# Block-sparse attention feeding a Swish MLP on one core: batch 0's block sums of V, both heads of a pair in one matmul

## The chip, the core and the metric

The kernel runs on one core of one Trainium2 chip. The core has five engines that work side by side: TensorE (PE) with its separate weight loads (PEld), VectorE (DVE), ScalarE (ACT), GpSimd (POOL) and SyncE (SP), and DMA queues. The metric is the device time of one execution in microseconds. The kernel before takes 212.0 us, the median of three runs (211.83 to 213.88).

## What is computed

An attention over four batches of eight heads (768 positions, 64 numbers per head) mixes a narrow window of near positions with 24 block summaries: the maximum of each block of 32 keys, and the mean of each block of 32 values. Its output goes through a two-layer MLP with a Swish between.

```python
    block, window = (32, 16)
    k_sum = k.reshape(B, H, nb, block, D).max(axis=3)
    v_sum = v.reshape(B, H, nb, block, D).mean(axis=3)
    ...
    scores_all = np.concatenate([scores_l_m, scores_s], axis=-1)
    ...
    v_all = np.concatenate([v, v_sum], axis=2)
    return np.matmul(a, v_all).astype(np.float32)
```

```python
    h = x @ w_in
    g = h * (1.0 / (1.0 + np.exp(-beta * h)))
    return (g @ w_out).astype(np.float32)
```

## The kernel before

Heads go in four pairs per batch. For each pair the values lie in `ve` as chunks of 128 rows, shifted by 16 positions, so that a head's 768 positions touch seven chunks (`NC = 7`; the two heads of a pair stand six chunks apart, `nch = 6`). The block sums of a head are seven matmuls, one per chunk, of the stationary matrix `A_avg[:, c]` (128 rows by 32 columns, a one where the row belongs to the block) with the chunk's 64 columns, accumulated in PSUM. Since the stationary matrix has 32 columns, such a matmul uses a strip of 32 of the PE array's 128 columns; `tile_position=(0, n)` says which strip, and the result lands on the 32 PSUM rows of that strip.

There are two routines for these sums. `mean_v` (L374) serves batches 1 to 3: it takes the two heads of a pair in one matmul (128 columns) and puts the four pairs on the four strips, chunk by chunk, 28 matmuls in all. `sum_v` (L384) serves batch 0 and takes one pair per call, because the pairs' values arrive one after the other in the first 20 us: 14 matmuls, head 0 and head 1 in turn, each on a strip of its own (strips 0 and 32 for pairs 0 and 2, 64 and 96 for pairs 1 and 3). Two copies per pair (L388, on DVE for pairs 0 and 1, on ACT for pairs 2 and 3) bring the sums from PSUM into `vd`, where head h of the pair has rows of its own. `blk0` (L466) multiplies `vd` with the block weights; `own0` (L454) and `edge0` (L460) add the near positions.

The order is written out by hand for the first stage: each engine does its work in the order of the calls, and an instruction that waits holds everything behind it on its engine. On PE that order is scores of pair 2, `sum_v(0)`, scores of pair 3, `sum_v(1)`, `own0` of pairs 0 and 1, `scores_blk(1)`, `blk0` and `edge0` of pairs 0 and 1, `sum_v(2)`, `own0`, `edge0`, `blk0` of pair 2, the small transpose of beta (L248), `sum_v(3)`, `own0(3)`, `edge0(3)`, `turn_x` (transposes, L491), `blk0(3)`, another `turn_x`, and then the first MLP matmuls (`h_dots`, L613). The values themselves are loaded by POOL's DMAs, one per pair (L116), ahead of the weights of the MLP.

From about 20 us on, PE goes from one block of matmuls to the next: the first MLP layer (L613, L643), the second (L664, L695), and between them the attention of the next batch (scores L508 and L525, values L570, sums L374).

Of the kernel before, what the change touches and what calls it, by code (L numbers as in the profile page):

```python
# [12 lines left out]
def kernel(  # L13
# [10 lines left out]
    nc = tc.nc  # L24
    ctx.enter_context(tc.manual_schedule(engines={getattr(mybir.EngineType, e) for e in ("SP", "Pool", "PE", "DVE", "Activation")}))
    P = 128
    f32 = mybir.dt.float32
# [4 lines left out]
    B, H, S, D = q.shape  # L32
# [4 lines left out]
    nch = S // P  # L37
    NC = nch + 1
# [41 lines left out]
    PC = 2 * nch  # L80
    ve_bufs = [const.tile([P, HC + 1, VW], bf16, name=f"ve{i}") for i in range(2)]
# [54 lines left out]
    A_avg = const.tile([P, NC, 32], bf16, name="A_avg")  # L136
# [7 lines left out]
    vd_bufs = [const.tile([P, 4, VW], bf16, name=f"vd{i}") for i in range(2)]  # L144
# [139 lines left out]
    def take(name, dt=f32):  # L284
        n = pools["n"]
        return pools["pool"].tile([P, n, 512 if dt == f32 else 1024], dt, name=name, tag="big", bufs=6 // n)
# [4 lines left out]
    def psum(shape, dt, name, tag):  # L291
        if tag == "t":
            return ps.tile(shape, dt, name=name, tag="t", bufs=2)
        flat = take(name, dt)[:, 0, 0:math.prod(shape[1:])]
        if len(shape) == 2:
            return flat
        return flat.rearrange("p (a b) -> p a b", b=shape[2])
# [80 lines left out]

    def sum_v(g, copy=dve):
        lo = HP * (g % 2)  # L380
        vm_ps = psum([P, D], f32, "vm_ps", "t")
        for c in range(NC):
            for h in range(2):
                nc.tensor.matmul(vm_ps[lo + 32 * h:lo + 32 * h + 32], A_avg[:, c], ve_bufs[0][:, PC * g + nch * h + c, 0:D],  # L384
                                 start=(c == 0), stop=(c == NC - 1), tile_position=(0, lo + 32 * h))
        for h in range(2):
            r = slice(lo + 32 * h, lo + 32 * h + 32)
            copy(out=vd_bufs[g // 2][r, 2 * (g % 2) + h, 0:D], in_=vm_ps[r])  # L388

    def rows_v0(g, copy=pool):  # L390
        for h in range(2):
# [318 lines left out]
    for nm, t, copy, src in (("k", qk_bufs["k"][:, 0:2], dve, k_f32), ("q", q0_bufs[0][:, 0:2], act, q_f32)):  # L710
        nat[(nm, 0, 0)] = t
        copy(out=t.rearrange("p h f -> p (h f)").rearrange("p (j h d) -> p h j d", h=2, d=D),
             in_=src.rearrange("p h (j d) -> p h j d", d=D))
# [17 lines left out]
    max_k(0, 2)  # L731
    scores0(2)
    sum_v(0)
    scores0(3)
    max_k(0, 3)
    sum_v(1)
    more_constants()
    open_av((0, 0, 2))
# [6 lines left out]
    edge0(1)  # L745
    norm_x((0, 0, 2))
    sum_v(2, act)
    open_av((0, 2, 1))
    own0(2, True)
# [81 lines left out]
    for b in range(B):  # L831
# [6 lines left out]
        main, t = [], 0.0  # L838
# [33 lines left out]
        if b == 0:  # L872
# [23 lines left out]
            for g in pairs:  # L896
                t = dn0 + OT * TK[g] if g < 2 else up1 + TK[g]
# [15 lines left out]
        elif nxt < B:  # L913
            for g in pairs:
                t = (2.6, 6.5, 10.4, 14.3)[g]
# [60 lines left out]
```

## Time and profile before

| | before |
|---|---|
| three runs, median (lowest to highest) | 212.0 us (211.83 to 213.88) |
| the profiled execution, its own time | 212.08 us |
| its span, first to last instruction | 210.4 us |
| PE busy | 204.0 us, 97% of the span |
| DVE, ACT, POOL busy | 110.5, 118.6, 80.5 us |
| L384, the sums of batch 0 | 56 matmuls between 12.0 and 17.6 us |

The rows of the profile give an instruction's start in us from the span's first instruction, and what engine, line and tile it belongs to. A matmul's duration counts from its first column until its result is in, so matmuls that follow each other overlap in these rows; how fast they go is read from the distance of their starts.

### The profile page before, as it was taken

What the parts mean: (1) busy time and instruction counts of PE and PEld (TensorE: products, weight loads), DVE (VectorE), ACT (ScalarE), POOL (GpSimd) and SP (SyncE); (2) the same over time, 40 slices, a digit from 0 to 9 for tenths busy, and PEclk for the clock granted to TensorE, in tenths of its full rate; (3) what the DMA queues carried; (4) which work ended last, traced back from release to release, by engine and by line L of the source; (5) the groups of instructions that cost most, each with busy time, mean ns of one, the idle gap of its engine ahead of it and who ended that gap; (6) DMA issues with size and microseconds to landing.
All of it is one profiled execution on the core that took longest, in us unless ns stands there. A gap on an engine that the chain in (4) does not pass through costs nothing.

```text
span 210.4 us, 4961 instructions
## 1 busy us (share of the span) xinstructions
PE 204.0 (97%) x2044; PEld 113.1 (54%) x2044; DVE 110.5 (53%) x311; ACT 118.6 (56%) x170; POOL 80.5 (38%) x116
## 2 busy tenths in 40 slices
PE   7998999999999999999999999999999999999993
PEld 2566654456555556565555456655545565654452
DVE  4887998987959868323926667524425000002120
ACT  3684988159697386668336266669165176640000
POOL 7997997593063399676300092000000000000000
PEclk9999999999999999999999999999999999999999
DMA  6999999999949999999999899900342500001212
GB/s 158 170 154 206 201 204 203 193 155 226 142 73 157 125 182 134 148 151 153 157 191 151 128 153 151 185 13 0 118 110 76 152 2 3 0 0 51 100 53 100
DMA packets 92055, 26.46 MB, mean 126 GB/s; under 512 B 81136, under 2 KB 89088, under 8 KB 92032
## 3 DMA queue, kind: packets, MB, share of 16 engines
q0 software_dynamic: 63888, 13.34, 78.7%
q1 hardware_dynamic: 27792, 12.40, 32.4%
q10 hardware_dynamic: 352, 0.39, 0.6%
q8 instruction: 16, 0.26, 0.5%
q14 instruction: 7, 0.06, 0.1%
HBM read 27.27 MB, written 6.29 MB: 160 GB/s over the span
## 4 chain that ended last, share of the span: by engine, by line
PE 85%; DMA 8%; POOL 3%; DVE 1%; issue 0%; ACT 0%
PE o_ps L664 35%; PE h_ps L613 32%; PE o_ps L695 5%; DMA qt<-q_all 4%; DMA ve<-in_v_dram 4%; PE h_ps L643 4%; PE av_ps L570 3%; PE s_ps L525 2%; POOL ve L116 1%; PE s_ps L508 1%; PE px L491 1%; POOL q L103 1%; PE vm_ps L374 0%; DVE qt L309 0%; PE av_ps L560 0%; POOL near L155 0%
## 5 line engine op out<-in xcount | busy, mean ns | idle before, releaser
L613 PE MATMUL h_ps<-xT,w_in_sb 128*128 128x384 bf16 x464 | 76.7, 326 | 0.0
L664 PE MATMUL o_ps<-w_out_sb,h_sb 128*128 128x512 bf16 (+2 forms) x352 | 75.8, 370 | 0.0
L625 ACT ACTIVATE h_sb<-h_ps,beta_sb 128x768 bf16<-128x768 f32 (+1 forms) x80 | 59.2, 775 | 23.2 <-PE h_ps L613 19.4
L613 PEld LDWEIGHTS <-w_in_sb 128*128 128x128 bf16 x464 | 45.0, 98 | 29.8
L664 PEld LDWEIGHTS <-h_sb 128*128 128x128 bf16 x352 | 32.6, 98 | 35.6
L683 DVE COPY o_sb<-o_ps 128x512 f32<-128x512 f32 x5 | 3.5, 691 | 38.6 <-PE o_ps L664 38.6
L551 DVE TENSOR_TENSOR attn<-attn,band 128x768 bf16<-128x768 bf16 x24 | 13.0, 555 | 17.3 <-ACT attn L500 15.6
L683 ACT COPY o_sb<-o_ps 128x512 f32<-128x512 f32 x15 | 8.9, 596 | 22.4 <-PE o_ps L664 17.2
L110 POOL DMA_DIRECT2D q_all<-in_q_dram x24 | 20.1, 858 | 3.5 <-DMA ve<-in_v_dram 2.8
L500 ACT ACTIVATE attn<-s_ps 128x768 bf16<-128x768 f32 x24 | 17.7, 814 | 3.6 <-PE s_ps L525 2.2
L116 POOL DMA_DIRECT2D ve<-in_v_dram x16 | 16.6, 1053 | 5.1 <-DMA w_out_sb<-in_moe_w_out_dram 3.6
L110 POOL DMA_DIRECT2D k_all<-in_k_dram x16 | 13.7, 870 | 3.7 <-DMA ve<-in_v_dram 2.4
L346 DVE TENSOR_TENSOR half<-kw 128x384 bf16<-128x384 bf16 x16 | 5.8, 365 | 16.5 <-DMA kw<-k_all 16.4
L367 DVE COPY vo<-ve 64x780 bf16<-64x780 bf16 (+3 forms) x30 | 11.4, 381 | 0.7
L580 DVE TENSOR_TENSOR x_nat<-av_ps,r 128x768 bf16<-128x768 f32 x12 | 11.5, 957 | 0.5
L695 PE MATMUL o_ps<-w_out_sb,h_sb 128*128 128x512 bf16 x48 | 11.6, 380 | 0.1
L676 ACT COPY o_sb<-o_ps 128x384 f32<-128x384 f32 x1 | 0.5, 480 | 19.0 <-PE o_ps L664 19.0
L244 ACT ACT_TABLE_LOAD x7 | 9.0, 1283 | 0.1
L643 PE MATMUL h_ps<-xT,w_in_sb 128*128 128x384 bf16 x48 | 8.3, 326 | 0.0
L356 DVE COPY kw<-kw 128x192 bf16<-128x192 bf16 (+2 forms) x32 | 8.3, 306 | 0.0
L493 ACT COPY xT<-px 128x384 bf16<-128x384 bf16 (+1 forms) x5 | 3.0, 608 | 8.0 <-PE px L491 8.0
L403 DVE COPY vo<-vm 32x780 bf16<-32x780 bf16 x12 | 7.4, 616 | 0.2
(125 smaller groups left out, 193.8 us busy)
## 6 DMA issues: line engine op xcount, KB each, us to landing
out_dram<-o_sb SPq DMA_DIRECT2D x23, 256.0 KB, 3.1
ve<-in_v_dram POOLq DMA_DIRECT2D x12, 192.0 KB, 6.5
q_all<-in_q_dram POOLq DMA_DIRECT2D x24, 96.0 KB, 7.7
w_in_sb<-in_moe_w_in_dram POOLq DMA_DIRECT2D x8, 256.0 KB, 8.5
k_all<-in_k_dram POOLq DMA_DIRECT2D x16, 96.0 KB, 6.8
w_out_sb<-in_moe_w_out_dram POOLq DMA_DIRECT2D x4, 256.0 KB, 6.7
w_out_sb<-in_moe_w_out_dram POOLq DMA_DIRECT2D x2, 512.0 KB, 8.9
k_all<-in_k_dram POOLq DMA_DIRECT2D x5, 192.0 KB, 9.0
```

The costliest lines, as they stand in the source:

```text
L110: nc.gpsimd.dma_start(out=t[:, :, h], in_=(k_row if nm == "k" else q_row)[b, g, :, h])
L116: nc.gpsimd.dma_start(out=ve_bufs[b % 2][:, lo:hi, 0:D], in_=src)
L367: copy(out=dst, in_=src)
L500: nc.scalar.activation(out=at[(b, g)][:, par].rearrange("p m h f -> p h m f"), in_=sv, func=ACTF.Exp, scale=scale)
L551: nc.vector.tensor_mul(out=a, in0=a, in1=band[:, par])
L580: nc.vector.tensor_mul(out=x.rearrange("p m h d -> p h m d"), in0=ov[:, :, :, 0:D], in1=r[:, :, :, None].to_broadcast([P, 2, n, D]))
L613: nc.tensor.matmul(big[:, j, 0:MG], w_in_sb[:, ki, ni * P:(ni + 1) * P], xT[b][:, ki, tok:tok + MG], start=(ki == 0), stop=(ki == k1 - 1))
L625: nc.scalar.activation(out=hb.rearrange("p (k m) -> p k m", m=MG), in_=big[:, j:j + w, 0:MG], func=ACTF.Silu, scale=beta_sb[:, ni:ni + 1])
L643: nc.tensor.matmul(h_open[(u, i)][:, j, 0:MG], w_in_sb[:, ki, i * P:(i + 1) * P], xT[b][:, ki, t0 + j * MG:t0 + (j + 1) * MG], start=start ...
L664: nc.tensor.matmul(o_ps[:, c0:c1], h_bufs[(u, ni * w // k2)][:, ni % (k2 // w), ms * P:(ms + 1) * P], w_out_sb[:, ni, c0:c1], start=(ni == ...
L683: (act if u + 1 < len(units) else dve)(out=o_sb[:], in_=o_ps[:])
L695: nc.tensor.matmul(o_ps, h_bufs[(u, ni * w // k2)][:, ni % (k2 // w), ms * P:(ms + 1) * P], w_out_sb[:, ni], start=(ni == 0), stop=(ni == ...
```

## The change

`sum_v` takes both heads of a pair in one matmul per chunk: the moving operand is the chunk of head 0 and the chunk of head 1 (a step of `nch` chunks in `ve`), 128 columns together, and the result stands on 32 PSUM rows, head 0 in the first 64 columns and head 1 in the next 64. One strip is used per pair in place of two (strip 0 for pairs 0 and 2, strip 64 for pairs 1 and 3). The two copies read the same 32 rows; that of head 1 writes 32 rows further down than it reads.

```diff
     def sum_v(g, copy=dve):
         lo = HP * (g % 2)
-        vm_ps = psum([P, D], f32, "vm_ps", "t")
+        vm_ps = psum([P, 2, D], f32, "vm_ps", "t")
         for c in range(NC):
-            for h in range(2):
-                nc.tensor.matmul(vm_ps[lo + 32 * h:lo + 32 * h + 32], A_avg[:, c], ve_bufs[0][:, PC * g + nch * h + c, 0:D],
-                                 start=(c == 0), stop=(c == NC - 1), tile_position=(0, lo + 32 * h))
+            col = PC * g + c
+            nc.tensor.matmul(vm_ps[lo:lo + 32], A_avg[:, c], ve_bufs[0][:, col:col + nch + 1:nch, 0:D],
+                             start=(c == 0), stop=(c == NC - 1), tile_position=(0, lo))
         for h in range(2):
-            r = slice(lo + 32 * h, lo + 32 * h + 32)
-            copy(out=vd_bufs[g // 2][r, 2 * (g % 2) + h, 0:D], in_=vm_ps[r])
+            r = lo + 32 * h
+            copy(out=vd_bufs[g // 2][r:r + 32, 2 * (g % 2) + h, 0:D], in_=vm_ps[lo:lo + 32, h])
```

The order of the engines' work stays. The waits of `sum_v` move a little. On PE, where `sum_v(3)` begins (the transpose of beta stands ahead of it; `DMASW0_49` is the semaphore of the load of pair 3's values, `PE_49` that of PE's own finished matmuls), the rows before are:

```order
L248 MATMUL beta_ps<-identity_103,beta_tmp 128x16 [waits DMAHW3_49,DVE_49]
L384 LDWEIGHTS A_avg
L384 MATMUL vm_ps<-ve_78,A_avg 32x64
L384 LDWEIGHTS A_avg
L384 MATMUL vm_ps<-ve_78,A_avg 32x64 [waits DMASW0_49]
L384 LDWEIGHTS A_avg
L384 MATMUL vm_ps<-ve_78,A_avg 32x64
```

and of the change, at the same place:

```order
L248 MATMUL beta_ps<-identity_103,beta_tmp 128x16 [waits DMAHW3_49,DVE_49,PE_49]
L384 LDWEIGHTS A_avg [waits DMASW0_49]
L384 MATMUL vm_ps<-ve_78,A_avg 32x128 [waits PE_49]
L384 LDWEIGHTS A_avg
L384 MATMUL vm_ps<-ve_78,A_avg 32x128
```

The wait for the load stands one matmul earlier, since the first matmul now reads both heads, and a wait for PE's own earlier matmuls stands at the transpose of beta and at the first matmul of the sums; `own0(3)` behind them no longer has one.

## Rows read from the trace of the kernel before

**Rows 1.** The page: busy time of PE, and the granted clock in 40 slices.

```profile
PE 204.0 (97%) x2044; PEld 113.1 (54%) x2044; DVE 110.5 (53%) x311; ACT 118.6 (56%) x170; POOL 80.5 (38%) x116
PEclk9999999999999999999999999999999999999999
```

**Rows 2.** The chain that ended last, in order of time: start us, us, what.

```profile
6.20 3.04 POOL ve L116 x3
9.24 7.94 DMA ve<-in_v_dram
...
17.22 0.38 PE vm_ps L384 x13
...
48.45 0.07 PE pk L308
48.52 9.28 DMA qt<-q_all
...
57.93 0.53 PE s_ps L508 x24
...
207.23 0.29 DVE o_sb L676
```

**Rows 3.** Timeline of PE, 8 to 20 us: start us, us, engine, instruction, count.

```profile
11.97 0.39 PE L384 MATMUL vm_ps<-ve,A_avg 128*32 128x64 bf16 x14
12.30 0.58 PE L420 MATMUL s_ps<-neg_m,identity 128*128 128x480 bf16 x2
...
13.12 0.40 PE L384 MATMUL vm_ps<-ve,A_avg 128*32 128x64 bf16 x14
13.45 0.54 PE L454 MATMUL av_ps<-ve,attn 128*128 128x65 bf16 x12
...
16.65 0.20 PE L384 MATMUL vm_ps<-ve,A_avg 128*32 128x64 bf16 x1
17.22 0.38 PE L384 MATMUL vm_ps<-ve,A_avg 128*32 128x64 bf16 x13 [0.37 <-DMA ve<-in_v_dram]
17.54 0.35 PE L454 MATMUL av_ps<-ve,attn 128*128 128x65 bf16 x6
```

**Rows 4.** The tile vm_ps: count, ns of one (least/median/most), first and last start.

```profile
L374 PE MATMUL vm_ps<-ve,A_avg x84: 217/220/230, 54.5 to 122.6; 128*32 128x128 bf16 x84
L384 PE MATMUL vm_ps<-ve,A_avg x56: 189/194/203, 12.0 to 17.4; 128*32 128x64 bf16 x56
```

**Rows 5.** Timeline of PE, 54 to 58 us: the sums of batch 1.

```profile
54.48 0.58 PE L374 MATMUL vm_ps<-ve,A_avg 128*32 128x128 bf16 x28
54.99 2.77 PE L613 MATMUL h_ps<-xT,w_in_sb 128*128 128x384 bf16 x16
```

**Rows 6.** Timeline of PE, 8 to 20 us again: between and after the sums.

```profile
15.55 0.36 PE L460 MATMUL av_ps<-ve,attn 128*32 128x65 bf16 x6
15.85 0.24 PE L466 MATMUL av_ps<-vd,ablk 128*128 128x65 bf16 x2
16.26 0.30 PE L466 MATMUL av_ps<-vd,ablk 128*128 128x65 bf16 x4 [0.18 <-issue]
...
18.11 0.51 PE L491 MATMUL px<-identity,x 128*128 128x128 bf16 x6
```

**Rows 7.** Timeline of ACT, 12 to 18.6 us: the copies of pair 3's sums.

```profile
17.62 0.44 ACT L388 CAST vd<-vm_ps 32x64 bf16<-32x64 f32 x2 [1.80 <-PE vm_ps L384]
```

**Rows 8.** Line L396, which spreads vd over other rows: ns of one (least/median/most).

```profile
L396 DVE COPY ve<-vd x6: 249/252/254, 25.5 to 29.8; 32x195 bf16<-32x195 bf16 x6
L396 DVE COPY vo<-vd x6: 246/249/253, 25.8 to 30.1; 32x195 bf16<-32x195 bf16 x6
```

**Rows 9.** Waits of PE: us in total, times, longest.

```profile
PE s_ps L508 <- DMA qt<-q_all: 0.2, 1, 0.2
```

**Rows 10.** Timeline of all engines, 46 to 60 us: POOL's loads and SP's transposes.

```profile
45.26 4.15 POOL L110 DMA_DIRECT2D q_all<-in_q_dram  x5
48.52 10.54 SPq L340 DMA_TRANSPOSE qt<-q_all  x4
```

## The prediction

> **What bounds the kernel now.** I read the page's busy times first: PE is busy 204.0 of 210.4 us, and its granted clock stands at the top in every slice, the 2.4 GHz level [rows 1]. So only time that PE loses or wins on the way to the end counts. Next comes the chain of work in order of time, to see where the sums of batch 0 lie on it. Three of the four calls of `sum_v` are not on it. What is: POOL issues the loads of the values up to 9.24 us, the last of them lands 7.94 us later, and at 17.22 the 13 remaining matmuls of `sum_v(3)` start on it; from there the chain goes on over PE to the end, with one stretch over a DMA, the transposes of q that PE releases at 48.45 and waits for at 57.93 [rows 2]. Then the timeline of PE around 12 to 18 us. Before 16.65 PE goes from one call to the next; there it issues the first matmul of `sum_v(3)`, and the next one starts at 17.22 because pair 3's values aren't there: 0.57 us between two starts that would else lie some hundredths apart [rows 3]. This hole is the cover of everything that PE does ahead of it.
>
> **What is removed and added.** Each call loses 14 matmuls of 64 columns with their weight loads and gets 7 of 128 columns. The columns that pass are the same, 896 per pair; the question is whether the 14 went one after the other.
>
> Before: the call at 11.97 lasts 0.39 us and one matmul takes 0.194 [rows 3, 4], so the last starts 0.39 - 0.19 = 0.20 us after the first, and the 13 steps between are 15 ns each. 64 columns at 2.4 GHz are 27 ns. So two matmuls do run at once, one head on each strip; in rounds of two it is seven rounds, 6 steps of 33 ns. A single strip goes at that same pace: six matmuls of 65 columns at L460, all on one strip and each with a new weight load, last 0.36 us with 0.19 for one, so 5 steps in 0.17, 34 ns [rows 6]. The strip sets the pace, with 6 to 7 ns over the columns' own time, and the second strip was free.
>
> After: seven matmuls of 128 columns on one strip. The trace shows this very operation, on four strips at once: `mean_v` at 54.48, 28 matmuls in 0.58 us with 0.22 for one [rows 4, 5], so its seven rounds start within 0.36 us, 6 steps of 60 ns. One strip alone should go the same, since 128 columns are 53 ns and 6 to 7 come on top. From the first start to the next block's start it takes 54.99 - 54.48 = 0.51 us there; now the calls take 12.30 - 11.97 = 0.33, 13.45 - 13.12 = 0.33 and, from the landing, 17.54 - 17.22 = 0.32 [rows 3, 5]. `sum_v(2)`, whose matmuls mix with L460's on another strip, has the same 14 and is counted as the first two. So **each call gets 0.18 us longer, the last one 0.19**, and the change gives up the second strip for it.
>
> TensorE: Matmul & The Clock Gate, in the Trainium skill (Part 3, Packing small matmuls), says that matmuls on different column strips run at the same time, with starts about 4 ns apart; the 15 ns per matmul above agree, and by that rule too the change loses. Another rule of the same page (Wait — 56ns, not 53.3ns?) speaks the other way: starts never come closer than about 25 ns however few the columns. By it 14 matmuls would need 0.35 us and 7 of 128 columns (56 ns each) 0.39, an estimate of 0.04 us lost per call; the rows here contradict it across strips.
>
> **What of it reaches the end.** The first three calls add 3 x 0.18 = 0.54 us ahead of 16.65, so PE comes to `sum_v(3)` at 17.19 instead of 16.65, and the landing lets it start at 17.22. They cost nothing, with 0.03 us of cover left. Without that cover they would cost all 0.54. What waits for the first sums moves with them: the copies and `blk0` stand behind the same PE work that is later by as much. The fourth call starts with the landing as before (its wait stands one matmul earlier, and the matmul that went ahead at 16.65 now comes after it, which the 0.51 for all seven rounds contains) and ends 0.19 later. Its two copies on ACT start at 17.62 and end at 18.06, just ahead of the transposes at 18.11 [rows 6, 7], which reuse PSUM space; they too begin 0.19 later, so the transposes come at 18.30 by either way.
>
> The copies: two of 32x64 as before, that of head 1 now writing 32 rows below the rows it reads. The rows show no such copy out of PSUM. The nearest are L396's, of which half move their rows to other ones and half do not, and all take 246 to 254 ns [rows 8]: I take zero. The bound above is a copy that takes twice its 0.22, so 0.2 us once, on ACT's way to the transposes; below, zero. The waits that are added for PE's own matmuls are for results that have long been there; the worst, at the first matmul of `sum_v(3)`, would be for the transpose of beta just ahead, and ends about when the load lands: zero to 0.05.
>
> Bounds of the 0.19: below, zero, if 128 columns went at the 33 ns of 64; above 0.23, if each of the six steps took 66 ns, the 60 of L374 and once more the 6 that a strip adds to the columns.
>
> From 18.3 on, the delay is carried: PE waits at 57.93 for the transposes of q, but these are released by PE itself at 48.45 [rows 2], so wait and release move together. The sum: profiled execution 212.08 + 0.19 = 212.27; against the median of 212.0, which lies 0.08 below that execution, 212.19. **I predict 212.2 us.**
>
> **The rivals.**
> 1. *Absorbed.* The 0.2 us that PE waits at 57.93 [rows 9] takes the delay in, if the transposes of q hang on the loads and not on PE's release. Then 212.0. The chain speaks against it, 18%.
> 2. *Cover gone.* The hole of 0.57 us is used up to 0.03. The gap at 16.26, where PE waits for nothing that the profile shows (0.18 us idle, 0.37 from start to start, 15.89 to 16.26, against 0.03 to 0.04 of its neighbours) [rows 6], may come elsewhere once 56 instructions fewer are ahead of it, behind the landing, at up to 0.35; the copy may take 0.2 more; the load may land 0.5 earlier, which uncovers the first calls. Each adds a part, together up to 0.9: 212.4 to 213.1, 11%.
> 3. *Starts were the limit.* If PE could not start small matmuls faster than a single strip does, half as many starts would win: 14 x 34 ns less 7 x 60 is 0.06 us per call, 212.0 - 0.06 on the path = 211.9, and at best 13 steps of 15 ns become 7, 0.1 less. The floor that the Trainium skill gives in TensorE: Matmul & The Clock Gate is a rule of this kind, though its 25 ns would leave a loss of 0.04. The 0.20 us for 14 starts [rows 3] speak against it: 4%.
> 4. *The other side: a transpose slips.* SP's four transposes of q take 10.54 us together, 2.6 each, and start just while POOL still issues loads of q until 49.41 [rows 10]. If PE's release, 0.19 later, lets one load more get ahead of a transpose, PE waits up to 2.6 us more at 57.93: 214.8, over 1% slower. It decides when the slip is over 1.9 us, so nearly a whole transpose. Against it: 0.19 is small against 2.6, and waits and releases here follow PE: 6%.
>
> **How the numbers follow.** The forecast has 61%. A measurement of this kernel can tell about 1%, 2.1 us, from no change. Only rival 4 is beyond that on the slow side, 6%; on the fast side nothing I can price is, and I leave 2% for that; 92% lie within. The range goes from rival 3 with the spread of the two lower runs (211.83 to 212.0) and some more below, 211.6, to the top of rival 2, 213.1; outside is rival 4 and little else. The forecast's own range is 212.0 to 212.5.
>
> **What would show it.** L384 has 28 matmuls of 128 columns at about 220 ns, seven in 0.58 us, and the block behind starts 0.51 after the first. PE arrives at `sum_v(3)` at about 17.2 and its idle time before it is nearly gone, while the start itself stays near 17.22; L454 follows at 17.73, L491 at 18.30, and the span is 0.2 longer. I am wrong if seven matmuls start within 0.2 us, if `sum_v(3)` starts later than the landing allows, if a copy at L388 takes more than 0.25, or if PE's wait at 57.93 changes by more than 0.2.

## The result, and the profile after

The changed kernel takes 212.8 us in the median of 20 runs (211.92 to 215.92); the kernel before, run beside it, takes 211.7 (211.23 to 213.88). The medians lie 1.1 us apart. The ratio by which this text goes is taken from the executions in the chip's faster state alone (of the changed kernel's 20, the one of 215.92 us was in the slower state): 1.0043, with a 95% interval of 1.0028 to 1.0059, which is 0.9 us more, from 0.6 to 1.25. That is within 1% and inside the predicted range of 211.6 to 213.1; it is more than the 0.19 us of the sum, and 212.8 is above the forecast's own 212.0 to 212.5.

The profiled execution of the changed kernel took 212.09 us, 0.7 below its own median; that of before took 212.08, 0.4 above the median of its 20 runs. So these two profiles, laid side by side, show the parts of the change but not the 0.9 us. What the rest is had to be found by experiment.

The page of the changed kernel, busy time and the granted clock, to be read against [rows 1]; the last row is the DMA queue that loads instructions (packets, MB, share of the time of 16 DMA engines), of which more below:

```profile
PE 202.7 (96%) x1997; PEld 113.5 (54%) x2016; DVE 110.5 (53%) x311; ACT 118.6 (56%) x170; POOL 80.4 (38%) x116
PEclk9999999999999999999999999999999999999999
q8 instruction: 16, 0.26, 0.5%
```

The clock is at its top as before. The weight loads are 2016 in place of 2044, 28 fewer, as the change says. Of the matmuls the trace has 1997, since 19 records are missing; nine short "issue" gaps that it shows at L664, and one at L695, are put down to such holes.

The timeline of PE, 8 to 20 us (start us, us, engine, instruction), for [rows 3, 6]:

```profile
11.76 0.57 PE L384 MATMUL vm_ps<-ve,A_avg 128*32 128x128 bf16 x7
12.26 0.58 PE L420 MATMUL s_ps<-neg_m,identity 128*128 128x480 bf16 x2
...
13.11 0.57 PE L384 MATMUL vm_ps<-ve,A_avg 128*32 128x128 bf16 x7
13.61 0.54 PE L454 MATMUL av_ps<-ve,attn 128*128 128x65 bf16 x12
...
16.18 0.36 PE L466 MATMUL av_ps<-vd,ablk 128*128 128x65 bf16 x6
16.48 0.23 PE L248 MATMUL beta_ps<-identity,beta_tmp 16*128 16x16 f32 x1
16.88 0.57 PE L384 MATMUL vm_ps<-ve,A_avg 128*32 128x128 bf16 x7 [0.17 <-DMA ve<-in_v_dram]
17.39 0.36 PE L454 MATMUL av_ps<-ve,attn 128*128 128x65 bf16 x6
...
17.98 0.50 PE L491 MATMUL px<-identity,x 128*128 128x128 bf16 x6
```

A call now takes 12.26 - 11.76 = 0.50, 13.61 - 13.11 = 0.50 and 17.39 - 16.88 = 0.51 us to the next block's start, where 0.33, 0.33 and 0.32 stood. From the landing of pair 3's values to the transposes it is 17.98 - 16.88 = 1.10 us, before 18.11 - 17.22 = 0.89: 0.21 more. The landing itself came 0.34 earlier in this execution, and that hides the 0.21 in the times. The gap that [rows 6] showed inside L466 at 16.26 is absent: six matmuls in 0.36.

The tile vm_ps and its copies (ns of one: least/median/most), for [rows 4, 7]:

```profile
L384 PE MATMUL vm_ps<-ve,A_avg x28: 217/218/230, 11.8 to 17.2; 128*32 128x128 bf16 x28
L388 DVE CAST vd<-vm_ps x4: 211/220/226, 12.4 to 14.1; 32x64 bf16<-32x64 f32 x4
L388 ACT CAST vd<-vm_ps x4: 203/206/207, 15.7 to 17.7; 32x64 bf16<-32x64 f32 x4
```

The copy that shifts its rows costs what the other does. The chain that ended last, in order of time, for [rows 2]:

```profile
8.93 7.91 DMA ve<-in_v_dram
16.88 0.57 PE vm_ps L384 x7
...
91.47 8.17 DMA kw<-k_all
101.30 1.89 DVE attn L551 x4
103.23 0.57 PE av_ps L570 x23
```

The transposes of q at 48.5 are no longer on it, and PE goes on at 57 us without the wait of [rows 9]:

```profile
57.32 0.52 PE L508 MATMUL s_ps<-qt,kw 64*128 64x64 bf16 x24
```

In their place stands a transpose of k (`kw`) at 91.47, on which DVE and then PE's matmuls with the values (L570) hang. The end waits for other transposes than before: the first hint of where the time went. They land no later than before. The first operation on them, in the timeline of DVE, 98 to 104 us, of before and of the changed kernel:

```profile
99.70 0.36 DVE L346 TENSOR_TENSOR half<-kw 128x384 bf16<-128x384 bf16 x1 [3.29 <-DMA kw<-k_all]
99.66 0.36 DVE L346 TENSOR_TENSOR half<-kw 128x384 bf16<-128x384 bf16 x1 [3.14 <-DMA kw<-k_all]
```

But PE is 0.4 us ahead of before at 76 us (the sums of batch 2 start at 75.80 in place of 76.20), and here it loses that lead.

### The profile page after: what moved, and what is told of

Its sections match the earlier page's. It is cut to its first block, busy times and chain, and to the rows that moved or that the text cites. A ratio compares the mean times of both kernels' runs of the same rounds, so it can differ in the third digit from the quotient of the medians.

```text
span 210.3 us, 4887 instructions
## 1 busy us (share of the span) xinstructions
PE 202.7 (96%) x1997; PEld 113.5 (54%) x2016; DVE 110.5 (53%) x311; ACT 118.6 (56%) x170; POOL 80.4 (38%) x116
## 4 chain that ended last, share of the span: by engine, by line
PE 83%; DMA 10%; DVE 2%; POOL 1%; issue 1%; ACT 0%
PE h_ps L613 35%; PE o_ps L664 31%; PE o_ps L695 5%; DMA kw<-k_all 4%; PE h_ps L643 4%; DMA ve<-in_v_dram 4%; PE av_ps L570 2%; DMA k_f<-in_k_dram 2%; POOL ve L116 1%; PE s_ps L525 1%; DVE attn L551 1%; PE s_ps L508 1%; PE vm_ps L374 1%; PE px L491 1%; PE av_ps L560 0%
## 5 line engine op out<-in xcount | busy, mean ns | idle before, releaser
L613 PE MATMUL h_ps<-xT,w_in_sb 128*128 128x384 bf16 x464 | 76.8, 326 | 0.0
L664 PE MATMUL o_ps<-w_out_sb,h_sb 128*128 128x512 bf16 (+2 forms) x336 | 72.9, 369 | 1.8 <-issue 1.4
L613 PEld LDWEIGHTS <-w_in_sb 128*128 128x128 bf16 x464 | 45.0, 98 | 29.8
L664 PEld LDWEIGHTS <-h_sb 128*128 128x128 bf16 x352 | 32.6, 98 | 35.6
L110 POOL DMA_DIRECT2D k_all<-in_k_dram x16 | 13.7, 872 | 3.6 <-DMA ve<-in_v_dram 1.9
L695 PE MATMUL o_ps<-w_out_sb,h_sb 128*128 128x512 bf16 x45 | 11.1, 380 | 0.3 <-issue 0.2
L676 ACT COPY o_sb<-o_ps 128x384 f32<-128x384 f32 x1 | 0.5, 480 | 19.0 <-PE o_ps L664 19.0
L643 PE MATMUL h_ps<-xT,w_in_sb 128*128 128x384 bf16 x48 | 8.5, 326 | 0.0
L356 DVE COPY kw<-kw 128x192 bf16<-128x192 bf16 (+2 forms) x32 | 7.7, 286 | 0.0
L570 PEld LDWEIGHTS <-attn 128*64 128x64 bf16 x288 | 5.3, 111 | 3.7 <-issue 1.7
```

Source lines behind the costliest of these rows:

```text
L110: nc.gpsimd.dma_start(out=t[:, :, h], in_=(k_row if nm == "k" else q_row)[b, g, :, h])
L613: nc.tensor.matmul(big[:, j, 0:MG], w_in_sb[:, ki, ni * P:(ni + 1) * P], xT[b][:, ki, tok:tok + MG], start=(ki == 0), stop=(ki == k1 - 1))
L643: nc.tensor.matmul(h_open[(u, i)][:, j, 0:MG], w_in_sb[:, ki, i * P:(i + 1) * P], xT[b][:, ki, t0 + j * MG:t0 + (j + 1) * MG], start=start ...
L664: nc.tensor.matmul(o_ps[:, c0:c1], h_bufs[(u, ni * w // k2)][:, ni % (k2 // w), ms * P:(ms + 1) * P], w_out_sb[:, ni, c0:c1], start=(ni == ...
L695: nc.tensor.matmul(o_ps, h_bufs[(u, ni * w // k2)][:, ni % (k2 // w), ms * P:(ms + 1) * P], w_out_sb[:, ni], start=(ni == 0), stop=(ni == ...
```

## The experiments

Each kernel was timed in five rounds beside the kernel before. The theories go by letters in the expectations. **A**: only the call behind the landing counts, 0.2 us. **B**: all four calls count, since PE often comes to `sum_v(3)` after the landing, 0.7. **C**: the 56 instructions fewer on PE move a stall in which PE lacks instructions. **D**: the arrangement before is a lucky one, and any disturbance of the first 20 us costs. **E**, formed after the first two groups: the loads that bring PE's own instructions run over the DMA engines; 56 instructions fewer move them in the program, into the transposes that PE waits for. In the table an instruction is a matmul or a weight load.

| run | what | instructions of PE against before | ratio to before (95%) |
|---|---|---|---|
| e1_same | the change once more | -56 | 1.0038 (1.0021 to 1.0054) |
| e2_pad | the change, filled up at the start | 0 | 1.0033 (1.0014 to 1.0052) |
| e3_first3 | new sums for pairs 0 to 2 | -42 | 1.0040 (1.0023 to 1.0058) |
| e4_last | new sum for pair 3 | -14 | 1.0054 (1.0033 to 1.0074) |
| b0_null | the kernel before | 0 | 1.0004 (0.9977 to 1.0031) |
| b1_warm10 | before, one more warming matmul | +2 | 1.0008 (0.9985 to 1.0031) |
| d3_delay3 | before, calls 1 to 3 later | +30 | 1.0033 (1.0004 to 1.0062) |
| d4_delay4 | before, all calls later | +40 | 1.0028 (0.9997 to 1.0059) |
| f1_after_pad28 | the change, filled up at 20 us and later | 0 | 1.0004 (0.9983 to 1.0026) |
| f2_before_pad100 | before, 200 more | +200 | 1.0037 (1.0012 to 1.0062) |
| f3_before_pad128 | before, 256 more | +256 | 1.0000 (0.9980 to 1.0020) |

**The change again, and its instructions filled up.** `e1_same` is the changed kernel without an edit.

> The changed kernel as it is, once more beside the kernel before. Theory A (only the call behind the landing counts): +0.2 us. Theory B (the values of pair 3 land earlier in most executions than in the profiled one, the hole ahead of sum_v(3) is shorter, and all four calls count): +0.7 us. Theory C (56 PE instructions fewer move the places where PE's instructions are loaded, and a stall falls on the path): +0.9 us as measured. In the profile: a wait of PE ahead of sum_v(3) of 0.1 us or more under A, none under B; a gap of PE without a cause elsewhere under C.

`e2_pad` is the changed kernel with more warming matmuls at the start (L714), so that what follows the sums stands at the count that it had before:

```diff
-    keep_warm(9)
+    keep_warm(37, 124)
```

> The changed kernel with the nine warm-up matmuls of 512 columns at the start cut into 37 of 124, the same columns, so that PE has as many instructions ahead of sum_v(3), and in all, as the kernel before. Theory C: the loss goes back to about +0.2 us. Theories A and B: as the changed kernel, unless the small matmuls take PE past 5.5 us, which the timeline shows.

`e1_same` took 212.42 us against 211.59, +0.8: the loss is real and repeats. `e2_pad` took 212.23, +0.7, which looks as if the count didn't matter. Its trace says otherwise. The instruction loads between 10 and 12.5 us (packets, MB, share), of which before has none there:

```profile
q8 instruction: 1, 0.02, 3.2%
```

and the timeline of PE in the same run:

```profile
12.11 0.57 PE L384 MATMUL vm_ps<-ve,A_avg 128*32 128x128 bf16 x7
14.12 0.57 PE L384 MATMUL vm_ps<-ve,A_avg 128*32 128x128 bf16 x7 [0.61 <-DMA ve<-in_v_dram]
```

The warming matmuls bring the first load forward from 13.7 to 11.1 us, among the loads of the values, and PE waits 0.61 us for pair 1's, which land at 14.07 in place of 13.07. So `e2_pad` pays elsewhere. Laid beside `b1_warm10`, its matmuls are 1.12 us later at 18 us and 1.04 at the end: behind the first stage it loses nothing more. Its loads there lie near those of before (62.6 for 62.2, 80.9 for 81.3 us). So it speaks against neither C nor E.

**Parts of the change.** Two kernels mix the routines: `sum_v_old` is the code before.

```diff
-    sum_v(3, act)
+    sum_v_old(3, act)
```

> The one matmul for both heads for pairs 0, 1 and 2 alone; pair 3 is summed as before. Theory A: 0.0 us against the kernel before, since the three calls lie in the hole. Theory B: +0.5 us. Theory C: between, 42 instructions fewer.

```diff
-    sum_v(0)
+    sum_v_old(0)
...
-    sum_v(1)
+    sum_v_old(1)
...
-    sum_v(2, act)
+    sum_v_old(2, act)
```

> The one matmul for both heads for pair 3 alone; pairs 0, 1 and 2 are summed as before. Theory A: +0.2 us, all of the loss. Theory B: +0.2 us, a quarter of it. Theory C: small, 14 instructions fewer. In the profile L454 of pair 3 follows 0.51 us after the start of sum_v(3).

`e3_first3` took 212.18 us against 211.59, a ratio of 1.0040, so it has the whole loss without the one call on which A put everything: A alone falls. Its profile shows a place. Timeline of PE, 56 to 59 us (here L519 is what L508 is in the others):

```profile
55.70 1.63 PE L624 MATMUL h_ps<-xT,w_in_sb 128*128 128x384 bf16 x9
58.27 0.53 PE L519 MATMUL s_ps<-qt,kw 64*128 64x64 bf16 x24 [0.95 <-DMA qt<-q_all]
```

and all engines, 46 to 60 us:

```profile
48.07 11.67 SPq L340 DMA_TRANSPOSE qt<-q_all  x4
```

The transposes of q stand in SP's queue for 11.67 us in place of the 10.54 of [rows 10], and PE's wait is 0.95 in place of 0.16. PE released them as ever; they ended later. An instruction load, 1.4 us long, ran at 55.5.

`e4_last` took 212.65 (7 runs), but the edit changed more than the sum: three transposes go ahead of a copy where six do in the others, and PE waits longer for that copy, 0.57 us in place of 0.2. Why this mix of old and new sums brings it, and that of `e3_first3` doesn't, isn't shown. The wait row of PE:

```profile
PE px L502 <- ACT xT L504: 0.6, 1, 0.6
```

In the same profile PE loses another 1.1 us at 103, at the transposes of k (in the table further down). The run decides nothing on the theories.

**The kernel before, disturbed.** `b0_null` is the kernel before against itself. `b1_warm10` has a tenth warming matmul at the start:

```diff
-    keep_warm(9)
+    keep_warm(10, 460)
```

> The kernel before itself, as a kernel of its own: what two equal kernels differ by, and a second profile of it. All theories: 0.0 us. In the profile the load of pair 3's values lands earlier than 17.18 if the first profile was late in this.

> The kernel before with its nine warm-up matmuls of 512 columns cut into ten of 460: two PE instructions more, no other work. Theories A and B (PE's time around the sums): 0.0 us. Theory D, new (the kernel before has a lucky arrangement, any change of its instructions loses it, by PE's instruction loading): +0.8 us, as the four kernels of the first call, which all lost 0.7 to 1.1 whichever calls were changed.

They took 211.71 and 211.76 us against 211.60. D falls for an edit of that kind: two instructions more and other times at the start change nothing that can be measured. What `b0_null` does show is the gap of [rows 6]; the wait row of PE, the timeline there, and the start of the transposes in `b0_null` and, last, in `b1_warm10`:

```profile
PE av_ps L466 <- issue: 0.5, 1, 0.5
```

```profile
16.06 0.24 PE L466 MATMUL av_ps<-vd,ablk 128*128 128x65 bf16 x2
16.80 0.30 PE L466 MATMUL av_ps<-vd,ablk 128*128 128x65 bf16 x4 [0.50 <-issue]
18.10 0.50 PE L491 MATMUL px<-identity,x 128*128 128x128 bf16 x6
17.60 0.51 PE L491 MATMUL px<-identity,x 128*128 128x128 bf16 x6
```

It was 0.18 in before's profile, is 0.50 here, and is absent in `b1_warm10`, `d3_delay3` and `d4_delay4`; in `f3_before_pad128` the six matmuls take 0.60 us in place of 0.36, so a hole of 0.24 stands there too, without a row of its own. In before's profile the gap lies ahead of pair 3's landing and costs nothing. In `b0_null` it costs: the values had landed at 16.59, PE came to the sums at 17.18, and the transposes start half a microsecond later than in `b1_warm10`. The profiles of the new sums for pairs 0 to 2 (`e1_same`, `e2_pad`, `e3_first3`, `f1_after_pad28` and the changed kernel) don't have the gap, so against such executions of before they save what the gap costs.

`d3_delay3` and `d4_delay4` are the kernel before with five more small matmuls ahead of the sums, about 0.17 us per call, of pairs 0 to 2 or of all. They lengthen the calls as the change does and add instructions instead of taking some away:

```diff
         lo = HP * (g % 2)
         vm_ps = psum([P, D], f32, "vm_ps", "t")
+        for _ in range(5 if g < 3 else 0):
+            nc.tensor.matmul(vm_ps[lo:lo + 32], A_avg[:, 1], ve_bufs[0][:, PC * g + 1, 0:D],
+                             start=True, stop=False, tile_position=(0, lo), skip_group_check=True)
```

> The kernel before, with five matmuls more ahead of the sums of pairs 0, 1 and 2 each (64 columns, one strip, their result is overwritten): some 0.17 us of PE a call, as the change adds, with 14 matmuls and two strips as before. Theory A: 0.0 us (the hole hides it). Theory B (PE's time counts, all of it): +0.5 us. Theory D: +0.8 us.

> As the one before, with the five matmuls ahead of the sums of all four pairs, those of pair 3 behind the landing of its values. Theory A: +0.2 us. Theory B: +0.7 us, like the changed kernel. Theory D: +0.8 us.

They took 212.10 and 212.01 us, +0.7 (0.1 to 1.3) and +0.6 (-0.1 to 1.25) by the ratios. The timeline of PE in `d3_delay3` (L387 is the sums, L383 the matmuls that were added):

```profile
16.76 0.36 PE L469 MATMUL av_ps<-vd,ablk 128*128 128x65 bf16 x6
17.05 0.23 PE L248 MATMUL beta_ps<-identity,beta_tmp 16*128 16x16 f32 x1
17.21 0.40 PE L387 MATMUL vm_ps<-ve,A_avg 128*32 128x64 bf16 x14
```

PE came to pair 3's sums at 17.21 and found the values landed, at 17.02. In `d4_delay4` it came 0.27 after the landing (17.07 against 16.80), and in `e1_same`, the changed kernel, 0.22 after (16.79 against 16.57; timeline of PE):

```profile
16.79 0.57 PE L384 MATMUL vm_ps<-ve,A_avg 128*32 128x128 bf16 x7
```

Over the 13 profiles the landing lies between 16.57 and 17.18 us, and where PE comes without a wait it comes between 16.79 and 17.21 (17.64 in `e2_pad`). The hole of 0.57 in the profile of before is the long end of what happens, so a part of the first three calls, about 0.2 us, reaches the transposes in some executions. That is for B, as far as it goes. The times of the two kernels don't weigh B against E. Their 30 and 40 instructions more move the instruction loads too (that of 62.2 to 59.9 and 59.8, that of 81.3 to 77.2 and 77.9). The intervals reach down to 0.1 or below. And the profiles, at 211.65 and 211.82 us, show no loss: in both the transposes start at 18.13, before at 18.11.

**Moving the instruction loads alone.** PE's instructions come in loads that have a queue of their own in the trace. There are 16 of them in before, whose page has 2044 matmuls and as many weight loads, 4088 instructions, and 17 with 200 and with 256 more: about one for each 256 instructions, 0.26 MB / 16 = 16 KB each. With 56 instructions fewer, each later load falls at a later place of the program. By that queue's records the load of before at 53.5 us comes at 57.0 in the changed kernel (at 55.2 in `e1_same`), that at 62.2 at 65.7, that at 81.3 at 86.0. The window views show it; the instruction loads (packets, MB, share) in before, 51 to 54.5 us, with none in 54.5 to 58:

```profile
q8 instruction: 1, 0.02, 1.7%
```

and in the changed kernel, 54.5 to 58 us, with none in 51 to 54.5:

```profile
q8 instruction: 1, 0.02, 2.1%
```

1.7% of 16 engines over 3.5 us is 0.95 us on one engine, 2.1% is 1.2. SP issues the transposes of q from 48.5 us on; the first lands at 57.79, the last at 60.64, and PE waits for the first at 57.93. The load of before falls among them too, but earlier.

So three kernels move the loads without touching the sums. `f1_after_pad28` is the changed kernel with 28 MLP matmuls, from 20 us on, cut in two halves of the same columns: the count is that of before from there on. `f2_before_pad100` and `f3_before_pad128` are the kernel before with 100 and 128 matmuls more by the same means. 100 more are 200 instructions, and 200 = 256 - 56 puts the loads where the change puts them; 128 more are 256, one whole load, and put them where before has them. The edit, in `f1_after_pad28` (`cut_more` counts `more` down; in the other two, `more` begins with 100 or 128 and a matmul of L613 is cut in six):

```diff
+    more = [28]
...
-                nc.tensor.matmul(big[:, j, 0:MG], w_in_sb[:, ki, ni * P:(ni + 1) * P], xT[b][:, ki, tok:tok + MG],
-                                 start=(ki == 0), stop=(ki == k1 - 1))
+                w_p = MG // (1 + cut_more(1 if u == 0 and i > 1 and 0 < ki < k1 - 1 else 0))
+                for c in range(0, MG, w_p):
+                    nc.tensor.matmul(big[:, j, c:c + w_p], w_in_sb[:, ki, ni * P:(ni + 1) * P], xT[b][:, ki, tok + c:tok + c + w_p],
+                                     start=(ki == 0), stop=(ki == k1 - 1))
```

> The changed kernel with 28 of its early MLP matmuls (24 of L613 and 4 of L695, between 22 and 36 us) cut into two halves of their columns, so that PE has 28 matmuls and 28 weight loads more, as many as the kernel before from there on. The cut costs an estimated 0.1 us (transposes of 128 columns follow each other at 56 ns, 53 at 2.4 GHz, so some 3 ns for each matmul more). Theory E, new: PE's instructions are loaded 16 KB at a time over the DMA engines; 56 instructions fewer move the load at 52 to 53 us of the kernel before to 55 to 57 us, into the end of the transposes of q for which PE waits at 57 us, and others near 74 and 86 us; each costs PE up to 1 us. Theory E: +0.3 us against the kernel before (0.2 behind the landing, 0.1 for the cut), the loads back at 52 to 53 us, and no wait of PE over 0.1 us at 57, 74 and 102 us. Theory B (all four calls count, nothing else): +0.8 us.

> The kernel before with 100 matmuls and 100 weight loads more by cutting (20 matmuls of L613 into six parts): 200 instructions more, which puts the loads of 256 instructions where the changed kernel has them (200 = 256 - 56). The sums of V are as before. The cut costs an estimated 0.3 us. Theory E: +0.9 us (0.6 of it by the loads at 55 to 57, 73 and 86 us), PE waits at 57, 74 or 102 us. Theory B: +0.3 us, and no such wait.

> The kernel before with 128 matmuls and 128 weight loads more by cutting (24 of L613 into six, 8 of L695 into two): 256 instructions more, one whole load, so that the later loads stand in the program where the kernel before has them. The cut costs an estimated 0.35 us. Both theories: +0.35 us and no wait over 0.2 us at 57, 74 and 102 us; it is what the run before is to be compared with.

Instruction loads in `f1_after_pad28`, 51 to 54.5 us (none in 54.5 to 58):

```profile
q8 instruction: 1, 0.02, 1.8%
```

in `f2_before_pad100`, 54.5 to 58 us (none in 51 to 54.5):

```profile
q8 instruction: 1, 0.02, 2.1%
```

and in `f3_before_pad128`, 51 to 54.5 us (none in 54.5 to 58):

```profile
q8 instruction: 1, 0.02, 1.6%
```

The loads lie where they were meant to. The cuts, estimated at 0.1 to 0.35 us in the expectations, cost nothing that shows. The times: `f1_after_pad28` 211.98 us, ratio 1.0004; `f2_before_pad100` 212.69, 1.0037; `f3_before_pad128` 211.73, 1.0000, all against 211.79. The kernel before, with the old sums, takes on 0.8 us from matmuls that cost nothing when there are 28 more of them; and the changed kernel, with the new sums, is within 0.1 us (-0.4 to +0.55) of before when the loads are put back. That speaks for E and against B as the main part: where the instruction loads fall is worth about 0.8 us.

Where `f2_before_pad100` lost it in its profile, the timeline of PE, 72 to 78 us (L652 is the first MLP layer, L643 before):

```profile
73.48 1.46 PE L652 MATMUL h_ps<-xT,w_in_sb 128*128 128x384 bf16 x8
76.24 1.46 PE L652 MATMUL h_ps<-xT,w_in_sb 128*128 128x384 bf16 x8 [1.30 <-DMA xT<-x_nat]
```

and the same place in `f3_before_pad128`:

```profile
73.26 2.98 PE L652 MATMUL h_ps<-xT,w_in_sb 128*128 128x384 bf16 x16
```

PE waits 1.30 us for a transpose of x. Its chain, and the instruction load in 64.5 to 67.5 us, while SP issues these transposes (65.20 to 69.33):

```profile
68.10 8.10 DMA xT<-x_nat
```

```profile
q8 instruction: 1, 0.02, 5.1%
```

5.1% of 16 engines over 3 us is a load of 2.4 us on one engine. In `f1_after_pad28` and `f3_before_pad128`, whose load comes at 62, that window has none, and PE doesn't wait. Another load ran at 73.9, still ahead of the landing; which of the two held the transpose is open. The chain of `f1_after_pad28` has no DMA on it behind 17 us: from there PE follows itself to the end.

**Where the time goes in all 13 profiles.** The table has where the sums of batch 1 and of batch 3 start (L374, timeline of PE) and the distance between them. No edit touches what PE does in between. From the sums of batch 3 to the last copy (L676 in before) it is 85.0 us in every one.

| run | instructions of PE against before | sums of batch 1, of batch 3 (us) | distance (us) |
|---|---|---|---|
| before | 0 | 54.48, 122.22 | 67.74 |
| b0_null | 0 | 54.41, 121.86 | 67.45 |
| e2_pad | 0 | 55.00, 122.45 | 67.45 |
| f1_after_pad28 | 0 | 54.43, 121.88 | 67.45 |
| f3_before_pad128 | +256 | 54.45, 122.12 | 67.67 |
| b1_warm10 | +2 | 53.96, 121.41 | 67.45 |
| d3_delay3 | +30 | 54.25, 121.80 | 67.55 |
| d4_delay4 | +40 | 54.49, 121.94 | 67.45 |
| the changed kernel | -56 | 54.10, 122.14 | 68.04 |
| e1_same | -56 | 54.26, 122.31 | 68.05 |
| e3_first3 | -42 | 54.04, 122.50 | 68.46 |
| e4_last | -14 | 54.82, 123.38 | 68.56 |
| f2_before_pad100 | +200 | 54.67, 123.58 | 68.91 |

Each is one execution. Still, the five with fewer instructions, or with the 200 more that shift the loads like 56 fewer, take 68.04 to 68.91 us, the other eight 67.45 to 67.74, whichever sums they have. PE waits in the five for the transposes of q (`e3_first3`, `e1_same`), of x (`f2_before_pad100`) or of k (`e1_same`, `e4_last`, the changed kernel). And since behind 20 us no profile has a gap of PE over 0.15 us without a releaser, the holes in the changed kernel's records aside, C as a stall of PE itself has no place there. `e4_last` fits E least: its loads lie near those of before (62.5 for 62.2, 82.8 for 81.3 us) and PE comes to batch 1 0.34 us later than in before. Which of the two brings its 1.1 us is open.

## Why the prediction was right, and where its size was off

**The cost of a call was right.** 0.17 us more per call were measured (0.50 against 0.33), and 0.19 for the last (0.51 against 0.32), where 0.18 and 0.19 were worked out, and 0.21 from the landing to the transposes where it was 0.19. 218 ns for one matmul and 0.57 for seven are the values taken from `mean_v`. A call with one strip in place of two takes half as long again. The rule of the Trainium skill that matmuls on different strips run at the same time (TensorE: Matmul & The Clock Gate, Part 3, Packing small matmuls) agrees with it.

**The copies at zero and the waits at zero were right.** The copies take 206 and 220 ns in the median, and no new wait on PE's own results stands in the list of waits.

**The cover of the first three calls came out by luck.** The prediction had PE come to `sum_v(3)` 0.54 us later than before. It came as early. The transpose of beta (L248), which stands just ahead, in before and in the changed kernel:

```profile
16.49 0.23 PE L248 MATMUL beta_ps<-identity,beta_tmp 16*128 16x16 f32 x1
16.48 0.23 PE L248 MATMUL beta_ps<-identity,beta_tmp 16*128 16x16 f32 x1
```

The calls were longer as predicted, but in this execution the first one began 0.21 earlier (11.76 against 11.97) and the gap of [rows 6], 0.34 us from start to start, was absent. And the cover had shrunk, since the values landed 0.34 earlier. PE's idle time ahead of `sum_v(3)` went from 0.37 to 0.17. The 0.57 was read from one execution. In `e1_same`, `e3_first3` and `d3_delay3` PE came after the landing, and then the calls ahead count. By its time, `f1_after_pad28` leaves from -0.4 to 0.55 us for all that the new sums change ahead of 20 us: the longer calls, the fourth call's 0.19 among them, less the gap of L466 where that is saved.

**The step that failed is "From 18.3 on, the delay is carried".** It took everything behind the sums as unchanged, because PE's work and its release of the transposes of q move together. They do; but how long the transposes take isn't fixed. From release to landing the first of q takes 9.28 us in before [rows 2] and 10.07 in `e3_first3`, further on those of x and k come late for PE, and the times tie this to where the instruction loads fall. That is the term which the sum lacked: about 0.8 us by `f1_after_pad28` against the changed kernel (ratios 1.0004 and 1.0043), and by `f2_before_pad100` against `f3_before_pad128` (1.0037 and 1.0000). With the 0.19 of the sum that makes 1.0, where 0.9 (0.6 to 1.25) was measured; the 0.19 is seen in the timeline and is too small for these times to tell.

**The range held by luck.** The forecast of 212.2 had its own range up to 212.5, and the 212.8 us lie above it. They are inside the whole range because room had been left there for the second rival, and none of that rival's three parts names what took most of the time.

**The rivals.** The first had the wait at 57.93 take the delay in. That wait hangs on the transposes, as it said: it is gone in the changed kernel's profile, 0.20 in `e1_same`, 0.95 in `e3_first3`, and 0.16 before. But no time was won by it; what PE is ahead there it loses at the transposes of k. The second gave the time that came, 212.4 to 213.1, and named the 56 instructions fewer, but it had the gap of 16.26 move behind the landing. That gap went away instead, and what the 56 instructions moved was loads 40 us and more behind. An earlier landing, its third part, did uncover the first calls in `e1_same`, by 0.22. The fourth named the right kind of thing, a transpose that slips, by another cause (a load of q that gets ahead), and at 2.6 us far too large. The third fell with the 0.50 per call.

**What is shown and what is argued.** Shown by times: shifting what follows by 56 instructions fewer, or 200 more, costs about what the change lost, with the old sums too, and shifting it back takes the loss away. Shown by the queue's records: the instruction loads shift with it. Shown in single profiles: PE waits for transposes, at 58 us in `e3_first3`, at 76 in `f2_before_pad100`, and at 103 in the changed kernel and `e1_same`. At 58 and 76 they land later than in before or `f3_before_pad128`; at 103 they land when those of before do, and PE loses its lead. Argued: that the load holds the transpose up on a DMA engine which both use; the trace gives the times of both but not what one waits for. Open: which of the loads costs how much in a typical execution, since the profiles lose it in different places; how much of the first three calls counts in a typical one; whether `d3_delay3` and `d4_delay4`, whose profiles show no loss, lost their 0.7 and 0.6 us to PE's work or to their loads; and the 1.1 us of `e4_last`.

The Trainium skill says of these loads (Runtime: NRT & Kernel Launch, Instruction fetch mechanics) that instructions come in blocks of 16 KiB, 256 of them, over a DMA queue of the sequencer's own, and that crossing a block's edge is mostly hidden. The 16 KB and the 256 agree with the rows above. Hidden they are for PE's own flow behind 20 us, where no gap without a releaser is seen, but where the edges fall is worth about 0.8 us of 212 here, and the profiles show such losses in waits for transposes.

## What to carry to other kernels

When an edit changes the number of an engine's instructions, look in the trace at which of the instruction loads move and what DMA transfers run there, above all those for which the busy engine waits or nearly waits; this edit lost some 0.4% by that. Before a small loss is put down to the edited work, fill the count up again with work that costs nothing, behind the edit and not at the start, and shift the unedited kernel by the same count. And a hole that is read as cover from one execution is one draw: take its size from several before a cost is hidden in it.

## What the runs showed of the hardware

- PE's instructions are loaded 16 KB at a time, 16 loads in this kernel, 0.9 to 1.9 us each, once 2.2 and once 2.4, and they run while transposes and loads do: shifting them by 56 instructions costs 0.8 us here (`f2_before_pad100` against `f3_before_pad128`, the changed kernel against `f1_after_pad28`), by 256 nothing (-0.4 to +0.4).
- A load that comes earlier may hurt as well: at 11.1 us in place of 13.7 it stood among the loads of the values, pair 1's landed 1.0 us later and PE waited 0.61 us for them (`e2_pad`, one profile; that the load held them up is argued).
- Cutting 24 matmuls of 384 columns into sixths and 8 of 512 into halves, each part with its weight load, 128 matmuls more in all, cost nothing that can be measured (ratio 1.0000, 0.9980 to 1.0020; PE busy 204.5 us against 204.0).
- The gap inside L466 without a releaser is 0.18 us in one execution of the kernel before, 0.50 in another, 0.21 in `e4_last` and 0.64 in `f2_before_pad100`. In these four the first instruction load comes at 13.5 to 13.9 us and is 1.0 to 1.6 long. Where that load comes earlier, at 11.1 to 13.3, the gap is absent, but for the hole of 0.24 in `f3_before_pad128` (load at 13.1); it is absent too in the changed kernel, whose first load came at 13.6 with 42 instructions fewer ahead of the place. That PE lacked its next instructions there is likely; it wasn't tried by itself.
